# Packed attention and a routed feed-forward: contiguous probabilities, v in three transfers, another order in the first batch

## The chip, the core and the metric

One core of a Trainium2 chip. The metric is device time in microseconds (us). The engines are PE (TensorE; PEld is its weight load), DVE (VectorE), ACT (ScalarE), POOL (GpSimd) and SP (SyncE, which only issues transfers here). Before the change the median of three runs is 465.64 us (465.35 to 465.92).

## The reference

Eight batches, eight heads, 576 positions of 64 elements, 32 packing queries `p` per head:

```python
def sm_attn(qq, kk, vv):
    s = scale * np.matmul(qq, kk.transpose(0, 1, 3, 2))
    a = softmax(s)
    return np.matmul(a, vv)
p_packed = sm_attn(p, k, v)              # 32 rows a head
out = sm_attn(q, p_packed, p_packed)     # 576 rows a head
x = out, heads joined: (4608, 512)
expert = argmax(normalized x @ normalized emb.T / tau)
y = gate * (relu(x @ w1[expert]) @ w2[expert])   # experts 512 -> 1024 -> 512
```

## The kernel before, in words

A batch is worked in two groups of four heads, g = 0 and 1. Its steps are: scores of the 32 packing queries against all keys (keys are turned in 32x32 blocks by DVE in `flip`, L268), their maximum (`key_max`, L326), exponential (`key_exp`, L330) and sum; the probabilities `p1` (128 rows of 4 heads x 32 queries, 576 columns) are transposed by PE in six pieces of 96 columns (`p1_turn`, L347), copied to SBUF (`p1_evac`) and multiplied with `v` (`pack_values`, L364). So in each piece the 96 keys on the partitions of `p1T` must be those on the partitions of the `v` tile. `flip` leaves column 32c + i for key 18i + c. `key_exp` then writes each column to the place of its key's number, a step of 18 elements apart, `p1_turn` takes every sixth column, and `load_v` (L189) puts the keys 6i to 6i + 5 on partition i, in one transfer of 96 partitions.

The packed rows give a second attention over all 576 queries (`att2`, L550): scores, a softmax in two halves of 288 columns (unpack, maximum, subtraction, exponential, sum, division, transpose, and a split of the result into a high and a low part), then routing (`route`, L661), counting (`counts`, L711) and gates (`gates`, L725). The expert of a batch is guessed (`guess`, L524) to load its weights early. The feed-forward (`ffn`, L822) takes w1 through the packed rows (G), then hidden matmuls (L868) in two halves of 8, whose results ACT and DVE take out of PSUM (L872, L873), 8 small steps for the last 64 rows (L895), and 4 x 8 steps of output matmuls (L913).

Engines execute their own queues in program order, and the program's order is written out: the feed-forward of batch b is a generator with a step per matmul group, and steps of batch b + 1's attention are put between (loop at L1295). Batch 0 has no feed-forward to hide behind. `begin` (L995) does its start: loads, scores, packing, the guess and the query scores of batch 0, then, step by step, batch 1's key scores and batch 0's packed rows and logits. `PLAN` (L1238) says which steps follow each step of batch 0's feed-forward: `q` is a step of `begin`, `s` of batch 0's softmax (its order is ORDS, L1230), `a` of batch 1's attention (`att_main`, L974, which takes `att1` with `pack_slowly`, L473), `G` and `w` split a piece of G and w2 into high and low parts, `r` is a step of batch 0's routing and counting, `g` of its gates. Entry 0 runs ahead of the feed-forward; entry n + 1 follows its step n: steps 0 to 11 are the first half of hidden with both parts of G (L836, L848), 12 to 19 the second half, 20 to 27 the small steps, 28 to 59 the output matmuls.

Transfers are issued by SP in program order (`nc.sync`), a few at the start by ACT, one by POOL, and weights of later batches by POOL. PSUM has three banks `pf` (`bank`, hidden, outputs), two double banks `pt` (`turn_bank`: scores, transposes, routing) and one `pu`. Batch 1's scores are made from POOL-scaled `wy` (L1034).

## Time and profile before

| | |
|---|---|
| median of three runs | 465.64 us |
| the profiled execution | 465.4 us, of which 463.8 are the span shown |
| PE busy | 439.3 us (95%) |
| DVE, ACT, POOL busy | 301.5, 211.9, 143.1 us |
| mean granted clock of PE | 0.984 |

The span is the time from the first to the last instruction. A busy PE is one with a matmul in flight, not one at its peak. The granted clock is a share of full speed: 1.00 is 2.4 GHz, and the lower level is 1.2 GHz. In a row of the timeline the brackets hold the idle time of the engine before the row and what ended it. A name like L334 is a line of the kernel, `pt<-ident,p` says what is written from what; names with q (SPq, ACTq) are an engine's queue when it issues a transfer.

### The profile page before, as it was taken

The page shows a single profiled execution, that of the slowest core. Times are in us where ns is not written, and L with a number is a line of the kernel's source. Part 1 is how long each engine was busy: PE and PEld are TensorE (multiplying, and loading weights), DVE is VectorE, ACT ScalarE, POOL GpSimd, SP SyncE. Part 2 cuts the span into 40 slices and gives each one's busy share as a digit, 9 for nine tenths or more (in the row PEclk, how much of TensorE's full clock was granted, in tenths as well). Part 3 has the DMA queues.
Part 4 walks back from the last instruction along what each step waited for, and adds up shares of the span by engine and source line. Part 5 has one row for each costly group of instructions (what it writes and reads, how often), then busy time and mean ns, then how long its engine had stood idle before and what let it go on. Part 6 is the DMA issues. An engine that isn't in the chain of part 4 may idle for free.

```text
span 463.8 us, 10721 instructions
## 1 busy us (share of the span) xinstructions
PE 439.3 (95%) x3926; PEld 345.2 (74%) x3927; DVE 301.5 (65%) x924; ACT 211.9 (46%) x478; POOL 143.1 (31%) x182
## 2 busy tenths in 40 slices
PE   6878979999999999999999999999999999999993
PEld 5544947768788796878788786878788796879783
DVE  4366858646895589846895589936895678735500
ACT  1447651366325651376325652276324662465210
POOL 1433663041521336040531326040531327023200
PEclk9899988999999999999999999999999999999998
DMA  7659768566597575876597656876587523710022
GB/s 205 217 197 290 207 178 290 183 168 181 152 365 204 153 216 194 295 191 176 153 342 228 175 164 200 299 209 173 158 320 213 168 69 108 291 47 23 14 47 50
DMA packets 39243, 87.11 MB, mean 188 GB/s; under 512 B 11144, under 2 KB 18568, under 8 KB 39184
## 3 DMA queue, kind: packets, MB, share of 16 engines
q1 hardware_dynamic: 30752, 56.85, 43.8%
q0 software_dynamic: 7872, 29.36, 17.2%
q8 instruction: 33, 0.54, 0.5%
q10 hardware_dynamic: 560, 0.15, 0.2%
q14 instruction: 26, 0.21, 0.1%
HBM read 76.89 MB, written 9.44 MB: 186 GB/s over the span
## 4 chain that ended last, share of the span: by engine, by line
PE 83%; ACT 6%; DVE 6%; issue 2%; POOL 1%; POOLq 0%; ACTq 0%; DVEq 0%
PE pf L913 37%; PE pf L868 18%; PE pf L895 7%; PE pt L672 7%; ACT p L334 4%; PE pt L251 3%; PE pt L801 3%; PE pt L367 2%; PE pt L350 2%; DVE mx L328 1%; ACT hT L872 1%; DVE hT L873 1%; PE pt L229 1%; PE pt L1082 0%; DVE at L609 0%
## 5 line engine op out<-in xcount | busy, mean ns | idle before, releaser
L913 PE MATMUL pf<-w2s,hT 128*128 128x512 f32 (+1 forms) x792 | 190.0, 391 | 0.9 <-ACT o L1207 0.9
L913 PEld LDWEIGHTS pf<-w2s,hT 128*128 128x128 f32 x792 | 142.9, 189 | 40.1 <-issue 9.5
L777 POOL TENSOR_TENSOR w2s<-w2r,w2s 128x512 fp32r<-128x512 f32 x64 | 82.2, 1288 | 239.6 <-ACT w2s L776 214.4
L868 PE MATMUL pf<-AT,G 128*128 128x288 f32 x720 | 106.4, 299 | 0.8
L868 PEld LDWEIGHTS pf<-AT,G 128*128 128x128 f32 x720 | 97.6, 188 | 7.5 <-issue 2.8
L873 DVE SCALAR_TENSOR_TENSOR hT<-pf,hT 128x224 fp32r<-128x224 f32 (+1 forms) x128 | 52.6, 415 | 38.7 <-ACT hT L872 38.6
L872 ACT ACTIVATE hT<-pf 128x224 fp32r<-128x224 f32 (+1 forms) x128 | 47.6, 384 | 46.9 <-PE pf L868 46.1
L272 DVE STREAM_TRANSPOSE kt<-nat 128x576 f32<-128x576 f32 x56 | 40.6, 752 | 1.4 <-DMA nat<-in_k 1.4
L688 ACT ACTIVATE at<-pt 128x512 f32<-128x512 f32 (+1 forms) x40 | 23.9, 598 | 36.2 <-DVE lg L681 35.5
L776 ACT CAST w2s<-w2r 128x512 fp32r<-128x512 f32 x64 | 39.2, 615 | 2.3 <-issue 1.2
L1207 ACT ACTIVATE o<-pf,gate 128x512 f32<-128x512 f32 (+1 forms) x41 | 26.0, 635 | 28.4 <-PE pf L913 17.5
L672 PEld LDWEIGHTS pt<-ppx,AT 128*128 128x128 f32 (+1 forms) x240 | 33.1, 177 | 5.6 <-issue 1.5
L672 PE MATMUL pt<-ppx,AT 128*128 128x264 f32 (+1 forms) x240 | 36.3, 287 | 0.0
L895 PE MATMUL pf<-w2r,h 128*64 128x256 f32 x256 | 35.0, 395 | 0.0
L815 DVE TENSOR_TENSOR G<-pt,G 128x512 fp32r<-128x512 f32 x28 | 18.8, 690 | 17.3 <-ACT G L814 17.3
L681 DVE TENSOR_REDUCE lg<-pt 128x8 f32<-128x16 f32 (+1 forms) x40 | 6.7, 167 | 35.4 <-PE pt L672 35.4
L588 ACT ACTIVATE st<-st 128x576 f32<-128x576 f32 (+1 forms) x17 | 11.2, 660 | 33.8 <-DVE st L585 33.1
L334 ACT ACTIVATE p<-pt,mx 128x576 f32<-128x576 f32 x16 | 21.4, 1337 | 9.6 <-DVE mx L328 9.6
L895 PEld LDWEIGHTS pf<-w2r,h 128*64 128x64 f32 x256 | 15.7, 137 | 9.6 <-issue 4.1
L766 POOL DMA_DIRECT2D w2r<-in_moe_w x28 | 19.8, 716 | 0.0
L615 ACT CAST AT<-at 128x576 fp32r<-128x576 f32 x16 | 10.8, 674 | 19.2 <-DVE at L609 19.2
L814 ACT CAST G<-pt 128x512 fp32r<-128x512 f32 x28 | 15.9, 589 | 7.3 <-DVE G L815 4.5
(184 smaller groups left out, 460.8 us busy)
## 6 DMA issues: line engine op xcount, KB each, us to landing
nat<-in_q SPq DMA_DIRECT2D x112, 140.0 KB, 3.1
w1t<-in_moe_w POOLq DMA_DIRECT2D x14, 1024.0 KB, 7.0
w2r<-in_moe_w POOLq DMA_DIRECT2D x28, 512.0 KB, 9.8
nat<-in_k SPq DMA_DIRECT2D x96, 140.0 KB, 3.1
vn<-in_v SPq DMA_DIRECT2D x16, 576.0 KB, 6.0
out<-o SPq DMA_DIRECT2D x124, 64.0 KB, 2.7
nat<-in_k SPq DMA_DIRECT2D x4, 576.0 KB, 7.3
w1t<-in_moe_w SPq DMA_DIRECT2D x4, 512.0 KB, 5.4
```

Source lines behind the costliest of these rows:

```text
L272: nc.vector.transpose(kt.rearrange("p (c i) -> p c i", i=32), t)
L334: nc.scalar.activation(x.p1[g].rearrange(order, f=2, i=32), s1_view(x, g).rearrange("p f (c i) -> p f c i", i=32), AF.Exp, bias=x.mx[g], a ...
L672: nc.tensor.matmul(pt[:r, 512 * g : 512 * g + XW], AT[:, a, g, c * P : c * P + r], x.ppx[:, m, g], start=(i == 0), stop=(i == 2),)
L688: nc.scalar.activation(scr[:r, :, : HB * D], ptv[:r, :, 0 : HB * D], AF.Square, accum_out=ss[:r, c : c + 1])
L776: nc.scalar.copy(t[:, 0], raw)
L777: nc.gpsimd.tensor_tensor(out=t[:, 1], in0=raw, in1=t[:, 0].bitcast(F32), op=ALU.subtract)
L868: nc.tensor.matmul(pf[:, :HS], w, r, start=(n == 0), stop=(n == len(ops) - 1))
L872: nc.scalar.activation(hT[:, 0, f, cs], pf[:, :n], AF.Relu)
L873: nc.vector.scalar_tensor_tensor(out=hT[:, 1, f, cs], in0=pf[:, :n], scalar=0.0, in1=hT[:, 0, f, cs].bitcast(F32), op0=ALU.max, op1=ALU.su ...
L895: nc.tensor.matmul(pf[64 * hf : 64 * hf + 64, :256], h4[:, f], x.w2r[f // 2][:, f % 2, hf * 256 : hf * 256 + 256], start=(f == 0), stop=(f ...
L913: nc.tensor.matmul(pf[:, :w], hT[:, a, f, c * P : (c + 1) * P], x.w2s[f][:, m, at : at + w], start=(f == 0 and i == 0), stop=(f == NF - 1 ...
L1207: nc.scalar.activation(o[:, :w], pf[:, :w], AF.Copy, scale=x.gate[:, c : c + 1])
```

## The change

`load_v` puts keys 18i + 6a to 18i + 6a + 5 on partition 32a + i, for a = 0, 2, 1 in three transfers of 32 partitions; in the first batch the one with a = 2 goes by ACT. For keys `flip` writes its 18 blocks in another order, so that each stretch of 96 columns belongs to one piece; `key_exp` writes straight, and `p1_turn` reads 96 neighbouring columns. In `begin` the small loads, the query transposes and batch 1's `wy` stand elsewhere, query transposes are copied in other pieces, and batch 1's keys are turned in the blocks' new order. PLAN is another from its third entry on.

```diff
--- before.py
+++ after.py
@@ -186,12 +186,14 @@
         return t
 
 
-    def load_v(b, g):
+    def load_v(b, g, odd=nc.sync):
         t = sb.tile([P, KC * HB * D], F32, name="vn", tag="vn", bufs=2)
         t = t.rearrange("p (h w) -> p h w", h=HB)
-        nc.sync.dma_start(
-            t[:KR], v[b, g * HB : (g + 1) * HB].rearrange("h (i c) d -> i h (c d)", c=KC)
-        )
+        s = v[b, g * HB : (g + 1) * HB].rearrange("h (i c) d -> i h (c d)", c=NCB)
+        for a in (0, 2, 1):
+            (odd if a == 2 else nc.sync).dma_start(
+                t[32 * a : 32 * a + 32], s[:, :, a * KC * D : (a + 1) * KC * D]
+            )
         return t.rearrange("p h (c d) -> p h c d", c=KC)
 
     def load_p(b):
@@ -265,11 +267,18 @@
         nc.scalar.copy(dst[0], src)
         eng.tensor_tensor(out=dst[1], in0=src, in1=dst[0].bitcast(F32), op=ALU.subtract)
 
-    def flip(t, e=0):
+    def flip(t, key, e=0):
 
         kt = sb.tile([P, S], F32, name="kt", tag="kq", bufs=8)
         t = t.rearrange("p (c e d) -> p c e d", e=2, d=32)[:, :, e]
-        nc.vector.transpose(kt.rearrange("p (c i) -> p c i", i=32), t)
+        if key:
+
+            nc.vector.transpose(
+                kt.rearrange("p (n a i) -> p a n i", n=KC, i=32),
+                t.rearrange("p (a n) d -> p a n d", n=KC),
+            )
+        else:
+            nc.vector.transpose(kt.rearrange("p (c i) -> p c i", i=32), t)
         return kt
 
     def packers(x, pn):
@@ -286,7 +295,7 @@
         packers(x, pn)
         yield
         for r in range(NPR):
-            x.kT[r] = flip(nat(r))
+            x.kT[r] = flip(nat(r), True)
             yield
 
 
@@ -330,11 +339,9 @@
     def key_exp(x, g):
         x.p1[g] = sb.tile([P, S], F32, name="p1", tag="p1", bufs=2)
         x.sums[g] = sm.tile([P, 1], F32, name="sums", tag="sums")
-        order = "p (i c f) -> p f c i" if x.halves else "p (i f c) -> p f c i"
         nc.scalar.activation(
-            x.p1[g].rearrange(order, f=2, i=32),
-            s1_view(x, g).rearrange("p f (c i) -> p f c i", i=32),
-            AF.Exp, bias=x.mx[g], accum_out=x.sums[g],
+            x.p1[g].rearrange("p (f s) -> p f s", f=2), s1_view(x, g), AF.Exp, bias=x.mx[g],
+            accum_out=x.sums[g],
         )
 
     def key_sum(x, g):
@@ -347,7 +354,7 @@
     def p1_turn(x, g, pt, pl=None):
         for c in range(KC):
             to = pl[:KR, (c - 4) * P : (c - 3) * P] if pl and c >= 4 else pt[:KR, c * P : (c + 1) * P]
-            nc.tensor.transpose(to, x.p1[g][:, c::KC], ident)
+            nc.tensor.transpose(to, x.p1[g][:, c * KR : (c + 1) * KR], ident)
 
     def p1_evac(x, g, pt, w=512, spare=None, pl=None):
 
@@ -367,7 +374,7 @@
                 nc.tensor.matmul(
                     pt[32 * at : 32 * at + 32, 0:D],
                     x.p1T[g][:KR, c, 32 * at : 32 * at + 32],
-                    vt[:KR, head(g, at), c, :],
+                    vt[:KR, head(g, at), c % 3 * 2 + c // 3 if x.halves else c, :],
                     start=(c == 0),
                     stop=(c == KC - 1),
                     tile_position=(0, 32 * at),
@@ -428,7 +435,7 @@
 
         def queries():
             for r in range(NPR):
-                x.qT[r] = flip(nat(NPR + r))
+                x.qT[r] = flip(nat(NPR + r), False)
                 yield
 
         def pack():
@@ -1001,13 +1008,13 @@
         pn = sm.tile([P, NG, D], F32, name="pn4", tag="pn4", bufs=1)
         nc.scalar.dma_start(pn, p[0].rearrange("(g h) j d -> (h j) g d", g=NG))
         next(emb_gen)
+        kn = [load_whole(k[0], g) for g in range(NG)]
+        vn = [load_v(0, g, nc.scalar) for g in range(NG)]
+        nc.scalar.dma_start(itau, tau.broadcast_to([P, 1]))
+        qn = [load_whole(q[0], g) for g in range(NG)]
         ny = sm.tile([P, NG, D], F32, name="pn", tag="pn")
-        nc.scalar.dma_start(ny, p[1].rearrange("(g h) j d -> (h j) g d", g=NG))
-        kn = [load_whole(k[0], g) for g in range(NG)]
-        vn = [load_v(0, g) for g in range(NG)]
-        qn = [load_whole(q[0], g) for g in range(NG)]
+        nc.sync.dma_start(ny, p[1].rearrange("(g h) j d -> (h j) g d", g=NG))
         kn1 = [load_whole(k[1], g) for g in range(NG)]
-        nc.gpsimd.dma_start(itau, tau.broadcast_to([P, 1]))
 
         def bank():
             return ps.tile([P, 512], F32, name="pf", tag="pf")
@@ -1031,25 +1038,15 @@
         nc.vector.transpose(
             pw[:, 1].rearrange("p g e j -> p (g e j)"), pw[:, 0].rearrange("p g e j -> p (g e j)")
         )
-        wy = sb.tile([P, 2, NG, 2 * D], F32, name="wy", tag="w2s", bufs=NF)
-        nc.gpsimd.tensor_scalar(
-            out=wy[:, 0].rearrange("p g (t d) -> p g t d", t=2),
-            in0=ny.unsqueeze(2).broadcast_to([P, NG, 2, D]),
-            scalar1=SCALE, scalar2=None, op0=ALU.mult,
-        )
         for g in range(NG):
             x.s1[g] = turn_bank()
             for e in range(2):
-                kt = flip(kn[g], e)
+                kt = flip(kn[g], True, e)
                 for hf in range(2):
                     quarters(x.s1[g], pw[:, 1, g, e], kt, lambda c: head(g, c), hf, hf, e)
             if g == 0:
                 for _ in range(3):
                     next(emb_gen)
-                pu = bank()
-                for h in range(NG):
-                    nc.tensor.transpose(pu[:, h * P : (h + 1) * P], wy[:, 0, h], ident)
-                nc.scalar.copy(wy[:, 1].rearrange("p g d -> p (g d)"), pu[:, : NG * P])
         key_max(x, 0)
         key_exp(x, 0)
         key_max(x, 1)
@@ -1077,23 +1074,19 @@
         qT, kT = turned[:, 0], turned[:, 1]
         x.Tw = sb.tile([P, NG * P], F32, name="tw", tag="w2s", bufs=NF)
 
-        def turn(nat, pt, at, n):
-            for i in range(at, at + n):
+        def turn(nat, pt, blocks):
+            for at, i in enumerate(blocks):
                 nc.tensor.transpose(
-                    pt[:, (i - at) * P : (i - at + 1) * P], nat[:, i * P : (i + 1) * P], ident
+                    pt[:, at * P : (at + 1) * P], nat[:, i * P : (i + 1) * P], ident
                 )
 
         def both_rows(g):
             nc.scalar.mul(rows2[:, g], po[g][:, :D].unsqueeze(1).broadcast_to([P, 2, D]), x.rinv[g])
 
         both_rows(0)
-        qa = turn_bank()
-        turn(qn[0], qa, 0, 2)
         po.append(bank())
         pack_values(x, 1, vn[1], po[1])
         pair_rows(x, 1, po[1])
-        turn(qn[0], qa[:, 2 * P :], 2, 6)
-        nc.scalar.copy(qT[:, 0, :1024], qa)
         drain(emb_gen)
         pt = pc.tile([P, 512], F32, name="pu", tag="pu")
         for g in range(NG):
@@ -1101,23 +1094,11 @@
                 pt[:, 2 * g : 2 * g + 2], x.pp2[g].rearrange("p s d -> p (s d)"), pairs,
                 start=True, stop=True,
             )
-        qb = turn_bank()
-        turn(qn[1], qb, 0, 4)
         total = sm.tile([P, NPR], F32, name="total", tag="total", bufs=1)
         nc.vector.tensor_scalar_mul(total, pt[:, :NPR], itau)
         both_rows(1)
         g_guess = guess(x, 0, mybir.EngineType.SP, total)
         next(g_guess)
-        turn(qn[1], qb[:, 4 * P :], 4, 4)
-        pu = bank()
-        for g in range(NG):
-            turn(qn[g], pu[:, g * P :], 8, 1)
-        nc.vector.tensor_copy(qT[:, 1, :512], qb[:, :512])
-        drain(g_guess)
-        load_w1(x, x.e, 2)
-        nc.scalar.copy(qT[:, 1, 512:1024], qb[:, 512:])
-        nc.scalar.copy(qT[:, :, 1024:], pu[:, : NG * P].rearrange("p (g s) -> p g s", g=NG))
-
         pu = bank()
         for g in range(NG):
             nc.tensor.transpose(
@@ -1131,6 +1112,17 @@
                 op=ALU.mult,
             )
         nc.scalar.copy(x.Tw, pu[:, : NG * P])
+        drain(g_guess)
+        load_w1(x, x.e, 2)
+        pu = bank()
+        for g in range(NG):
+            turn(qn[g], pu[:, g * P :], (8,))
+        nc.scalar.copy(qT[:, :, 1024:], pu[:, : NG * P].rearrange("p (g s) -> p g s", g=NG))
+        for g in range(NG):
+            for n, copy in enumerate((nc.scalar.copy, nc.vector.tensor_copy)):
+                pu = bank()
+                turn(qn[g], pu, range(4 * n, 4 * n + 4))
+                copy(qT[:, g, 512 * n : 512 * n + 512], pu)
 
         def parity_scores(to, w, t, g, at):
 
@@ -1156,15 +1148,25 @@
         load_w2(x, x.e)
         prefetch(order[1, NPR] + 3)
         yield
+        wy = sb.tile([P, 2, NG, 2 * D], F32, name="wy", tag="w2s", bufs=NF)
+        nc.gpsimd.tensor_scalar(
+            out=wy[:, 0].rearrange("p g (t d) -> p g t d", t=2),
+            in0=ny.unsqueeze(2).broadcast_to([P, NG, 2, D]),
+            scalar1=SCALE, scalar2=None, op0=ALU.mult,
+        )
         pu = bank()
         for g in range(NG):
-            turn(kn1[g], pu[:, g * P :], 8, 1)
+            nc.tensor.transpose(pu[:, g * P : (g + 1) * P], wy[:, 0, g], ident)
+        nc.scalar.copy(wy[:, 1].rearrange("p g d -> p (g d)"), pu[:, : NG * P])
+        pu = bank()
+        for g in range(NG):
+            turn(kn1[g], pu[:, g * P :], (8,))
         nc.scalar.copy(kT[:, :, 1024:], pu[:, : NG * P].rearrange("p (g s) -> p g s", g=NG))
         for n in range(2 * NG):
             if n >= NG:
                 yield
             pu = bank()
-            turn(kn1[n // 2], pu, n % 2 * 4, 4)
+            turn(kn1[n // 2], pu, [m % 3 * 3 + m // 3 for m in range(n % 2 * 4, n % 2 * 4 + 4)])
             nc.scalar.copy(kT[:, n // 2, n % 2 * 512 : n % 2 * 512 + 512], pu)
         yield
         y.halves = True
@@ -1236,13 +1238,13 @@
 
 
     PLAN = (
-        "qsssqsssssssqsqssqsssqs", "s", "as", "aq", "s", "aq", "sa", "sq", "sG", "sG",
-        "qa", "qa", "a", "aGGs", "as", "as", "aw", "aw", "aw", "a",
-        "wr", "ra", "ra", "rw", "rwg", "raw", "rwa", "ra", "arg", "ar",
-        "gaa", "agaaaag", "", "ragraaararga", "a", "gar", "gr", "", "rggr", "r",
-        "ra", "", "r", "gag", "gaga", "gagrar", "grara", "ag", "a", "grrgrar",
-        "rrraggg", "", "g", "rr", "ggaaagr", "ra", "aaga", "g", "r", "rg",
-        "arr",
+        "qsssqsssssssqsqssqsssqs", "s", "s", "G", "s", "G", "s", "s", "s", "sG",
+        "G", "", "aq", "a", "aq", "as", "aq", "aws", "aqs", "awq",
+        "aw", "awr", "awr", "ar", "awr", "awr", "aw", "ar", "g", "gr",
+        "gr", "gr", "ga", "ga", "gra", "gr", "gra", "ra", "a", "a",
+        "a", "a", "a", "a", "ga", "a", "a", "aa", "a", "a",
+        "aa", "a", "aa", "a", "aa", "aa", "aa", "aa", "aa", "aa",
+        "aa",
     )
     DBL = 8
     LAG = 2
```

## Rows read from the trace of the kernel before

**Rows 1.** The page, part 1: busy us, share of the span, instructions.
```profile
PE 439.3 (95%) x3926; PEld 345.2 (74%) x3927; DVE 301.5 (65%) x924; ACT 211.9 (46%) x478; POOL 143.1 (31%) x182
```
**Rows 2.** Stages: length, busy us (instructions) by engine, granted clock, DMA share, GB/s.
```profile
8.70:16.20 7.50, 4.26 (x36) 1.70 (x36) 2.08 (x4) 1.62 (x3) 3.69 (x16) 0.77 1.07 308
16.20:26.30 10.10, 7.16 (x148) 5.84 (x148) 5.10 (x19) 4.79 (x10) 2.81 (x3) 1.00 0.23 91
...
31.60:47.90 16.30, 13.85 (x100) 8.06 (x82) 10.94 (x24) 10.31 (x24) 6.04 (x7) 1.00 1.06 291
47.90:56.30 8.40, 8.40 (x150) 8.14 (x148) 6.79 (x24) 6.19 (x16) 5.80 (x5) 1.00 0.77 206
...
71.40:101.90 30.50, 29.64 (x165) 22.84 (x159) 20.72 (x57) 12.89 (x27) 7.89 (x11) 0.96 0.73 236
...
154.50:207.00 52.50, 52.03 (x478) 41.47 (x477) 38.28 (x111) 25.22 (x58) 16.28 (x20) 1.00 0.71 215
...
64.80:71.40 6.60, 3.80 (x47) 1.30 (x45) 4.14 (x18) 1.19 (x3) 4.79 (x7) 0.66 0.45 128
```
**Rows 3.** Timeline of PE, 155.5 to 175: start, us, operation, count, idle before.
```profile
156.64 4.59 PE L868 MATMUL pf<-AT,G 128*128 128x288 f32 x30
161.07 0.82 PE L350 MATMUL pt<-ident,p 128*96 128x128 f32 x6
162.22 0.91 PE L350 MATMUL pt<-ident,p 128*96 128x128 f32 x6 [0.33 <-ACT p L334]
162.88 5.29 PE L868 MATMUL pf<-AT,G 128*128 128x288 f32 x36
```
**Rows 4.** Waits of PE from 100 us on: total us, times, longest.
```profile
PE pt L350 <- ACT p L334: 2.0, 6, 0.3
```
**Rows 5.** Groups of ACT by shape: count, busy us, mean ns, idle before.
```profile
L334 ACT ACTIVATE p<-pt,mx 128x576 f32<-128x576 f32 x16 | 21.4, 1337 | 9.6 <-DVE mx L328 9.6
...
L588 ACT ACTIVATE st<-st 128x576 f32<-128x576 f32 x15 | 10.3, 686 | 33.8 <-DVE st L585 33.1 <-POOL st L585 0.7
```
**Rows 6.** Groups of PE's weight loads by shape, same columns.
```profile
L350 PEld LDWEIGHTS pt<-ident,p 128*96 128x96 f32 x94 | 11.5, 180 | 5.6 <-ACT p L334 4.8 <-issue 0.7
...
L396 PEld LDWEIGHTS pu<-ident,pp 128*128 128x128 f32 x14 | 1.9, 138 | 0.4
```
**Rows 7.** Groups of DVE by shape, same columns.
```profile
L272 DVE STREAM_TRANSPOSE kt<-nat 128x576 f32<-128x576 f32 x56 | 40.6, 752 | 1.4 <-DMA nat<-in_k 1.4
```
**Rows 8.** DMA issues, first 60 us: count, KB, median us to landing.
```profile
vn<-in_v SPq DMA_DIRECT2D x4, 576.0 KB, 10.8
```
**Rows 9.** Timeline of all engines, start of the kernel to the first hidden matmul.
```profile
6.56 2.14 PE L229 MATMUL pt<-kt,pw 32*32 32x288 f32 x32 [0.15 <-DVE kt L272]
...
11.02 0.87 POOL L1035 TENSOR_SCALAR wy<-pn 128x256 f32<-128x256 f32 x1 [8.43 <-DMA pn<-in_p]
...
12.31 3.81 PE L229 MATMUL pt<-kt,pw 32*32 32x288 f32 x32
...
26.27 1.21 PE L1141 MATMUL pt<-spare,tw 64*32 64x288 f32 x32 [1.51 <-ACT tw L1133]
26.39 2.14 SPq L758 DMA_DIRECT2D w1t<-in_moe_w  x4
...
29.28 0.46 ACT L588 ACTIVATE st<-st 128x288 f32<-128x288 f32 x1
...
33.42 1.24 PE L868 MATMUL pf<-at,g 128*128 128x288 f32 x4 [0.68 <-ACT g L848]
```
**Rows 10.** Waits of PE from 30 to 100 us.
```profile
PE pu L714 <- DVE m L420: 2.5, 1, 2.5
...
PE pf L913 <- ACT o L1207: 0.9, 1, 0.9
```
**Rows 11.** Timeline of DVE, 71 to 86: softmax of batch 1, first and last.
```profile
71.53 0.85 DVE L574 STREAM_TRANSPOSE st<-pt 128x288 f32<-128x288 f32 x2 [1.40 <-PE pt L251]
...
84.41 0.74 DVE L620 TENSOR_TENSOR AT<-at,AT 128x576 fp32r<-128x576 f32 x1
```

## Prediction, made before the changed kernel was run

> **What bounds the kernel now.** I read the busy shares first, then stages of the span, then PE's waits, then the timeline. PE is busy 95% of the span [rows 1], and PE's busy time alone does not say what an edit is worth, so the span is cut into stages [rows 2]. From 154.5 to 207.0 us, one batch, PE is busy 52.03 of 52.50 us at full clock: the other engines matter there only where they hold PE up, 0.47 us a batch. The first 102 us are different. From 8.70 to 16.20 PE is busy 4.26 of 7.50 us and the granted clock is 0.77; from 31.60 to 47.90 it has 2.45 us of plain idle time, with DVE at 10.94 and ACT at 10.31 us; from 64.80 to 71.40 it is idle 2.80 us and its clock is 0.66, which lasts into the next stage (0.96 over 30.5 us). So an edit pays either in the first batch's stages, or through the small hold-up in each later batch.
>
> The hold-up of later batches is seen on PE's timeline [rows 3]. Thirty matmuls of L868 start at 156.64 and the next stretch of L868 at 162.88, with twelve transposes of L350 between: 6.24 us. In the next stretch 36 matmuls take 5.29, 0.14 each, and a transpose follows another at (0.91 - 0.27)/5 = 0.13, so the same work would need about 30 x 0.14 + 12 x 0.11 to 0.13 = 5.5 to 5.8. What is lost is 0.5 to 0.75 us, of which 0.33 is a wait on the exponential of L334, the only wait for another engine that the waits of PE after 100 us name (2.0 us, 6 times) [rows 4].
>
> **The change part by part.**
>
> **Exponential (key_exp).** It has its output rows made contiguous; its input was already read in stretches of 288. It takes 1337 ns now, where the other exponential of the same 128x576, written without gaps, takes 686 [rows 5]. I take 0.65 us less, by that row; the bounds are 0 (if the writes were not the cause) and 0.75. A batch has two, each ahead of ReLUs on ACT that free PE's banks. The wait of 0.33 goes, and part of the bank waits in front of it: 0.33 to 0.75 a batch, I take 0.55. Batches 2 to 7 make 6 x 0.55 = 3.3 us. ACT's next late result would be the ReLU of L872, which then runs 0.65 us earlier.
>
> **Probability transposes.** Their weights were read with a step of six elements and become contiguous; the load takes 180 ns against 138 for a contiguous 128x128 [rows 6]. But the transposes follow each other at 0.11 to 0.13 us in either case, so I count nothing; bounds 0 and 12 x 0.04 = 0.5 us a batch.
> The Trainium skill (Advanced Engine Details and Errata, SBUF Cachelines) says that accesses which leave a 16-byte line each time pay a penalty. By it the 42 ns of each load would be saved, some 3 us over six batches; the pitch of the rows speaks against it.
>
> **Key flips.** 32x32 blocks are written at another place each, 28 flips in the main loop. The duration is 752 ns [rows 7]; bounds are no change and, if placement of blocks cost what the step cost the exponential, twice that. A block still writes 32 neighbours, as the contiguous case does: nothing.
>
> **v in three transfers.** Twelve transfers for every four of before, so about 0.4 us more of SP's issue each; 2 x 2 more a batch, 1.6 us on a queue that mostly waits for stores. PE waits for three landings in place of one. v lands 10.8 us after issue at the start [rows 8], is then needed at 14 us and later: I take nothing, bounds 0 and 1 us once. In the first batch one of three goes by ACT's queue, ahead of the activation of the embeddings, which has slack.
> At the start that piece, 2 x 192 KB, 0.39 MB, is in flight with the second half of the keys; at the 308 GB/s of 8.70 to 16.20 [rows 2] that is 1.3 us, so the keys come 0 to 1.3 us later; I take 0.5. The Trainium skill (DMA: Bandwidth & Descriptors, Issuing engines are not separate DMA queues) says that such transfers share one set of engines, so a second queue saves issue time alone: by it the delay is the full 1.3 us, and the sum would be 0.8 us worse.
>
> **Start.** Today POOL's scaling for batch 1 (L1035) waits for a small load until 11.02, PE waits for it, and the second group's 32 score matmuls then run from 12.31 in 3.81 us where the first took 2.14 [rows 9]. The scaling moves behind the first batch's query scores, so the second group ends at about 11.8 and not 16.1: 4.3 us. The exponential's 0.65 comes on top. The sixteen query transposes in front of the guess go behind it, 16 x 0.11 = 1.8 us at most. The weights' load, issued at 26.39, I expect at 19.7; the query scores, at 26.27, at 20.6, since the eighteen transposes and their five copies now stand directly ahead of them (2.4 us as I count it, ACT and DVE side by side). Then a new wait: the moved scaling stands on POOL behind the first half's subtraction, about 2 us after the scores, and PE's transposes of it, its copy and the copies of batch 1's keys stand on ACT ahead of the first softmax exponential. That one starts 3.0 us after the scores today (29.28) and I expect 5.5: 2.5 us given back. The first hidden matmul, at 33.42 today, comes at 30.4: **3.0 us**, bounds 1 and 5.5 (scaling fully hidden).
>
> **First batch, first half of hidden (31.6 to 47.9).** Batch 1's steps leave it: two maxima and small work, 2.9 us of DVE; two exponentials and copies, about 5.8 of ACT. What is left on DVE in order (two copies of G, eight hT, the second half's softmax, one split) comes to 9.2 us, and with the wait for POOL's subtraction at its head I get 12.2 us for the stage of 16.3. Twelve transposes and the logits, 2.2 us of PE's work, only move: **2.0 us**, bounds 0 and 3.
>
> **Second half of hidden.** Batch 1's steps come in here. Today ACT is busy 6.19 of 8.40 us [rows 2]; with two shorter exponentials, two copies of p1T and two splits of w2, it gets 9.3 against PE's 8.9: **1.0 us lost**, bounds 0 and 2.
>
> **Routing and after.** PE waits 2.5 us at L714 [rows 10], behind a copy of batch 1's logits; with batch 1's logits moved to later, and PE given two steps of L913 ahead of the counting, DVE's chain lies beside PE's work. Idle time 2.8 and the clock (3.80 us at 0.66, 30.5 at 0.96, so about 1.3 and 1.2) make 5.3; I take **4.6 us**, bounds 2 and 5.3. The gates are finished some three steps ahead of the first store, and the wait of 0.9 at L913 [rows 10] goes: **0.9 us**.
>
> **End of the first batch.** DVE's softmax of batch 1 takes from 71.53 to 85.15, 13.6 us [rows 11], with the keys' flips, 4 x 0.75 and the packers, 3.5 us, behind it. The new plan has about 19 steps of L913 between query scores and the first route matmul, at 0.72 us each 13.8 us. So DVE's softmax just fits, and the second routing matmuls wait for their banks behind the flips: 1.5 us, and 0.5 where G of batch 1 is ready late: **2.0 us lost**, bounds 0 and 5. Loads of batch 1's weights come later, but have over 15 us.
>
> **Sum.** 3.3 + 3.0 + 2.0 - 1.0 + 4.6 + 0.9 - 2.0 = 10.8 us. The profiled execution took 465.4 (span 463.8 and 1.6 around it), so 454.6; the median of the runs is 0.24 above it, so 454.9, said as 455.0.
>
> **The rivals.**
> - **The first batch gives nothing beyond its start.** Batch 1's chain, moved by ten steps, ends behind PE's work at the route, and eats what routing and gates gave. For it: 13.8 us of cover against 13.6 and more of DVE. Against it: DVE has pauses while ACT computes exponentials. Then 3.0 + 3.3 remain: 459.1. Chance 0.2.
> - **More than forecast.** POOL's scaling costs nothing, DVE fits: 2.5 + 2.0 + 1.0 more, 449.4. Chance 0.12.
> - **The exponential does not get faster,** so that the change doesn't do there what it says (its cost was the reading of two banks): 3.3 and some 0.7 of the start are gone: 459. Chance 0.05.
> - **Slower: the low clock.** The new start leaves PE with short bursts between 12 and 28 us, without the query transposes that fill it now. Today 8.70 to 16.20 was granted 0.77 after PE had next to nothing to do between 8.70 and 12.31, and the score matmuls took 1.78 times as long [rows 9]. PE has about 10 us of work on the chain from there to the first hidden matmul and 7 to 9 in the stage behind it; at the lower level of 1.2 GHz, by 0.78 us for each, that costs up to 8 and, half hidden, 4. With 12 lost against 10.8 the time is 466.8. It decides once the low clock covers nearly all of 10 to 40 us. Against it: 16.20 to 26.30, as loosely filled (7.16 of 10.10 us), had full clock [rows 2]. Chance 0.08.
> - Key flips at twice the time would add 3 us of DVE a batch to 38.28 of 52.50 [rows 2], which PE needs only partly: 462 to 468, chance 0.03.
>
> **How the numbers follow.** The forecast has 0.52. Its own bounds run from 449 to 460. The range takes in the first rival and the second nearly whole: 449.0 to 461.5, leaving out the slow cases and a little of the fast. About 0.2% is what a measurement of this kernel can tell from no change; faster 0.89 (the first four cases), slower 0.09 (the low clock and a third of the flips' case), same 0.02 (the rest of that case).
>
> **What would show it.** Right: L334 near 0.69 us; a batch's period near 52.0 and no wait at L350; the second group's scores done by 12 us; first w1 issue near 20; first hidden matmul near 30; ffn of batch 1 (hidden) starting near 95 where it starts at 101.9. Wrong: L334 unchanged, a low clock between 10 and 40 us, waits of PE for DVE at the routing of batch 1.

## The result, and the profile after

The changed kernel took 460.14 us as the median of four runs (458.36 to 460.86), the kernel before 465.72; the ratio is 0.9875, 95% interval 0.9847 to 0.9904. It is faster by 5.6 us, where 10.7 were forecast: inside the range, and half of what the sum promised. A second measurement (run after2 below) gave 0.985 [0.982, 0.988].

The profiled execution took 458.36 us, its span is 456.8, 7.0 shorter than before; it was the fastest of the four, and the one with the highest granted clock (0.988, the others 0.980 and 0.981). In the changed file most lines stand some seven further down: the exponential L334 is L342, the transposes L350 are L357, the hidden matmuls L868 are L875, the outputs L913 are L920, the key scores L251 are L253.

**Later batches.** First the groups by shape, of ACT, PE's weight loads and DVE (the columns of [rows 5]):
```profile
L342 ACT ACTIVATE p<-pt,mx 128x576 f32<-128x576 f32 x16 | 11.8, 741 | 7.3 <-DVE mx L337 7.3
...
L357 PEld LDWEIGHTS pt<-ident,p 128*96 128x96 f32 x94 | 10.4, 126 | 1.7 <-ACT p L342 1.1 <-POOL rq_t L109 0.6
...
L281 DVE STREAM_TRANSPOSE kt<-nat 128x576 f32<-128x576 f32 x28 | 21.3, 764 | 0.0
L276 DVE STREAM_TRANSPOSE kt<-nat 128x576 f32<-128x576 f32 x28 | 19.1, 736 | 0.0
```
The exponential fell from 1337 to 741 ns, the weight load from 180 to 126, and the key flips (L276), whose blocks now go elsewhere, cost no more than the query flips, which stayed. The timeline of PE, where [rows 3] answers:
```profile
154.39 4.21 PE L875 MATMUL pf<-AT,G 128*128 128x288 f32 x30
158.44 1.47 PE L357 MATMUL pt<-ident,p 128*96 128x128 f32 x12
159.67 5.29 PE L875 MATMUL pf<-AT,G 128*128 128x288 f32 x36
```
The stretch of 6.24 us is 5.28 now, and the wait inside it is gone. A whole batch, in the view of stages, is 51.60 where it was 52.50 [rows 2]:
```profile
152.30:203.90 51.60, 51.55 (x478) 41.44 (x478) 38.27 (x111) 24.48 (x59) 16.32 (x20) 1.00 0.73 219
```

**First batch.** Its stages, in the columns of [rows 2]:
```profile
28.40:41.70 13.30, 11.09 (x78) 6.59 (x58) 10.28 (x21) 7.34 (x15) 5.65 (x5) 1.00 1.03 271
41.70:52.50 10.80, 10.38 (x167) 9.53 (x165) 7.04 (x25) 8.82 (x26) 5.81 (x7) 1.00 0.45 132
52.50:61.60 9.10, 9.10 (x71) 5.75 (x64) 6.25 (x15) 5.68 (x16) 7.43 (x8) 1.00 0.23 67
61.60:93.60 32.00, 31.21 (x208) 23.04 (x207) 23.14 (x74) 11.99 (x27) 11.24 (x16) 1.00 0.88 272
93.60:101.20 7.60, 3.89 (x44) 1.72 (x42) 3.12 (x6) 2.45 (x5) 0.35 (x1) 0.79 0.63 173
101.20:111.20 10.00, 10.00 (x68) 9.99 (x66) 5.00 (x13) 5.04 (x14) 0.00 (x0) 0.82 0.37 107
```
The routing stage has full clock and hardly an idle PE. The loss sits in the last two rows: PE is busy only 3.89 of 7.60 us in the first, and the granted clock is 0.79 there and 0.82 in the next. All engines there, by the timeline:
```profile
91.95 6.19 SPq L1215 DMA_DIRECT2D out<-o  x9
...
93.64 0.95 PE L875 MATMUL pf<-AT,G 128*128 128x288 f32 x6
...
95.71 0.69 ACT L1209 ACTIVATE o<-pf,gate 128x512 f32<-128x512 f32 x1 [1.73 <-DMA out<-o]
96.30 0.58 ACT L821 CAST G<-pt 128x512 fp32r<-128x512 f32 x1
96.91 0.69 DVE L822 TENSOR_TENSOR G<-pt,G 128x512 fp32r<-128x512 f32 x1 [2.79 <-ACT G L821]
97.63 0.59 ACT L821 CAST G<-pt 128x512 fp32r<-128x512 f32 x1 [0.76 <-DVE G L822]
98.11 0.42 ACT L879 ACTIVATE hT<-pf 128x288 fp32r<-128x288 f32 x1
...
98.86 0.18 DVE L726 TENSOR_REDUCE cnt<-pu 1x8 f32<-1x40 f32 x1
...
99.08 2.15 PE L253 MATMUL pt<-kt,pw 64*32 64x288 f32 x24 [3.71 <-DVE cnt L726]
...
101.16 5.86 PE L875 MATMUL pf<-AT,G 128*128 128x288 f32 x30
```
Read it upwards from the last row but one. PE waits 3.71 us for the counts of L726, a small reduction that DVE could have done at 94.8. It stands on DVE's queue behind two subtractions for G (L822), these wait for ACT's copies (L821), and ACT had been waiting 1.73 us for an output buffer: there are two, and a store had not left yet. Why not, SP's own queue tells:
```profile
83.65 5.42 SPq L178 DMA_DIRECT2D nat<-in_q  x12
89.18 1.32 SPq L194 DMA_DIRECT2D vn<-in_v  x3
90.59 7.55 SPq L1215 DMA_DIRECT2D out<-o  x12
```
Fifteen loads for a later batch stand ahead of the stores. An output that ACT had copied at 83.09 left from 90.59 on, and its buffer was the one ACT wanted at 94. In the kernel before the same kind of loads stands ahead of the stores too:
```profile
87.49 5.47 SPq L178 DMA_DIRECT2D nat<-in_q  x12
...
93.53 12.86 SPq L1213 DMA_DIRECT2D out<-o  x16
```
But no output copy of ACT waited more than 0.24 us there: the outputs came later against the queue (the third copy at 95.70, here at 83.09).

**The balance of the 7.0 us.** The hidden matmuls of batch 1 start 8.3 us earlier (93.64 against 101.93). The stretch of 30 hidden matmuls shown above, in the second batch after, is only 2.25 earlier (154.39 against 156.64): 6.0 were given back between. That is a net figure, since a batch's gain by the shorter exponential, some 0.95, lies in this stretch too, so 7.0 were lost in it: 3.7 by the wait above; 2.6 by the lower clock (the 24 score matmuls took 2.15 us, 1.17 at full clock in the run drain below, and the thirty hidden matmuls behind them 5.86, where the thirty shown above took 4.21); 0.7 is not traced further. The batches behind it, five of the six that gain, then add 4.75.

### The profile page after: what moved, and what is told of

It is laid out like the page before. It is cut to its first block, busy times and chain, and to the rows that moved or that the text cites. A ratio compares the mean times of both kernels' runs of the same rounds, so it can differ in the third digit from the quotient of the medians.

```text
span 456.8 us, 10781 instructions
## 1 busy us (share of the span) xinstructions
PE 434.9 (95%) x3926; PEld 345.6 (76%) x3927; DVE 302.9 (66%) x925; ACT 204.9 (45%) x478; POOL 142.6 (31%) x181
## 4 chain that ended last, share of the span: by engine, by line
PE 84%; DVE 6%; ACT 4%; DMA 2%; issue 1%; POOL 1%; SPq 0%; ACTq 0%; DVEq 0%; POOLq 0%
PE pf L920 36%; PE pf L875 22%; PE pf L902 6%; PE pt L679 6%; PE pt L253 3%; PE pt L808 2%; PE pt L374 2%; PE pt L357 2%; DMA pn<-in_p 1%; DMA out<-o 1%; DVE kt L276 1%; ACT p L342 1%; DVE hT L880 0%; DVE at L616 0%; PE pt L231 0%
## 5 line engine op out<-in xcount | busy, mean ns | idle before, releaser
L920 PE MATMUL pf<-w2s,hT 128*128 128x512 f32 (+1 forms) x792 | 189.2, 390 | 0.0
L920 PEld LDWEIGHTS pf<-w2s,hT 128*128 128x128 f32 x792 | 142.0, 188 | 38.3 <-issue 9.4
L875 PE MATMUL pf<-AT,G 128*128 128x288 f32 x720 | 106.9, 302 | 0.7 <-DVE h L885 0.4
L875 PEld LDWEIGHTS pf<-AT,G 128*128 128x128 f32 x720 | 99.2, 191 | 6.7 <-issue 3.2
L879 ACT ACTIVATE hT<-pf 128x224 fp32r<-128x224 f32 (+1 forms) x128 | 48.6, 385 | 49.5 <-PE pf L875 48.1
L822 DVE TENSOR_TENSOR G<-pt,G 128x512 fp32r<-128x512 f32 x28 | 18.9, 690 | 17.9 <-ACT G L821 17.9
L595 ACT ACTIVATE st<-st 128x576 f32<-128x576 f32 (+1 forms) x17 | 11.2, 660 | 31.1 <-DVE st L592 30.4
L281 DVE STREAM_TRANSPOSE kt<-nat 128x576 f32<-128x576 f32 x28 | 21.3, 764 | 0.0
L746 ACT ACTIVATE lg<-lg 128x40 f32<-128x40 f32 x8 | 1.9, 237 | 39.6 <-DVE lg L742 39.6
L821 ACT CAST G<-pt 128x512 fp32r<-128x512 f32 x28 | 15.9, 588 | 7.4 <-DVE G L822 4.8
```

What stands on the lines that cost most here:

```text
L281: nc.vector.transpose(kt.rearrange("p (c i) -> p c i", i=32), t)
L875: nc.tensor.matmul(pf[:, :HS], w, r, start=(n == 0), stop=(n == len(ops) - 1))
L879: nc.scalar.activation(hT[:, 0, f, cs], pf[:, :n], AF.Relu)
L920: nc.tensor.matmul(pf[:, :w], hT[:, a, f, c * P : (c + 1) * P], x.w2s[f][:, m, at : at + w], start=(f == 0 and i == 0), stop=(f == NF - 1 ...
```

## The experiments

The line numbers in these rows are those of each kernel's own file, and ratios are against the kernel before on the same chip.

**1 and 2. The layout alone, the order alone.** layout is the kernel before with the contiguous exponential, key flips by the new index and v in three pieces on SP; order_only is the change without these.
```diff
-            x.p1[g].rearrange(order, f=2, i=32),
-            s1_view(x, g).rearrange("p f (c i) -> p f c i", i=32),
-            AF.Exp, bias=x.mx[g], accum_out=x.sums[g],
+            x.p1[g].rearrange("p (f s) -> p f s", f=2), s1_view(x, g), AF.Exp, bias=x.mx[g],
+            accum_out=x.sums[g],
...
```


> The kernel before with the contiguous probability rows, the new flips and v in three transfers (all by SP), and nothing else. Theory: the exponential alone makes each later batch shorter, 51.6 us a batch where before has 52.5, and the start by about 0.7 us; so 5.4 to 6.5 us less than before, 459.2 to 460.3. Rival: three transfers for one of v delay what stands behind them on SP, and eat part of it: a period over 52.0 and a time of 462 or more.

> The changed kernel with the old probability layout, the old flips and v in one transfer: only the start and the plan are new. Theory: period 52.5 as before; the first batch reaches the first hidden matmul of batch 1 some 6 to 7 us earlier than before (before 101.9), and gives most of it back in the wait behind the output stores and the low clock after it: 463.5 to 466. Rival: the three transfers of v in front of the stores on SP make that wait, so with one transfer it is gone or under 1.5 us, and the time is 461 or less.

Measured: layout 457.57 us, ratio 0.983 [0.979, 0.987], below the range expected of it: its start came 1.8 to 2.5 us earlier and not 0.7, and the rest of the first batch gained 2 us too (66.5 and 66.7 from its first hidden matmul to batch 1's in two profiles, 68.5 before); order_only 465.59, 0.999 [0.997, 1.002], as expected. The measured gain is the layout's. Not that the order did nothing on its way: in order_only batch 1's hidden matmuls start at 94.11, 7.8 us early, and then PE stands still and the clock falls (timeline of PE, then the stage from 90 to 110 us):
```profile
100.01 1.67 PE L251 MATMUL pt<-kt,pw 64*32 64x288 f32 x20 [4.17 <-DVE cnt L719]
```
```profile
90.00:110.00 20.00, 15.52 (x134) 11.14 (x133) 8.71 (x21) 10.12 (x22) 2.59 (x2) 0.83 0.58 153
```
v is loaded in one piece there, so the pieces did not make the stall.

**3. G's copies ahead of the last stores (drain).** The changed kernel, with two lines at the end of the first batch:
```diff
+        if late:
+            drain(after.w1g)
         for t in last:
             store(*t)
```


> The changed kernel, but at the end of the first batch's feed-forward the copies of batch 1's G are put ahead of the last two output stores on ACT and DVE. Theory: the stall of PE at batch 2's key scores (3.7 us) comes from ACT, which waits 1.7 us for an output buffer with two of G's copies behind it; it falls under 1 us, the clock stays up behind it, and the time falls by 4 to 6.5 us to 453.6 to 456. Rival: G is late because batch 1's steps end late in the plan; then the wait stays over 2.5 us and the time within 1 us of the changed kernel's 460.1.

Measured: 455.13, 0.977 [0.973, 0.981]. PE's timeline and the same stage:
```profile
97.99 1.17 PE L253 MATMUL pt<-kt,pw 64*32 64x288 f32 x24 [0.83 <-DVE cnt L726]
```
```profile
90.00:110.00 20.00, 19.12 (x201) 15.36 (x204) 12.94 (x36) 13.18 (x34) 4.70 (x4) 1.00 0.70 188
```
The wait is 0.83 and the clock full. From the start of batch 1's hidden matmuls to the next hidden stretch, after the key scores, it is 3.67 us (95.42 to 99.09) where the changed kernel needs 7.52. As the theory had it: the order of ACT's queue, with the buffer wait at its head, was the stall.

**4. The exponential with gaps again (strided_exp).** All else as in the change; its transposes read contiguous rows, so the probabilities meet rows of v that are not theirs. That leaves the same work.


> The changed kernel with the exponential writing its columns 18 apart again, while the transposes of the probabilities read neighbouring columns; the probabilities then meet rows of v that aren't theirs. Theory: the exponential's duration makes the gain of a later batch: L342 back at 1.34 us, period 52.4 to 52.6, time 465 to 467. Rival: the transposes' weight loads (180 ns to 138) carry a good part: period under 52.2 although the exponential is slow, time under 464.

Measured: 464.58, 0.996 [0.994, 0.999]. ACT's and the weight loads' groups, and a batch:
```profile
L343 ACT ACTIVATE p<-pt,mx 128x576 f32<-128x576 f32 x16 | 21.4, 1338 | 8.4 <-DVE mx L337 8.4
...
L359 PEld LDWEIGHTS pt<-ident,p 128*96 128x96 f32 x94 | 10.2, 126 | 5.5 <-ACT p L343 4.4 <-POOL ery L117 1.1
```
```profile
162.60:215.10 52.50, 52.04 (x478) 41.44 (x478) 38.29 (x112) 25.25 (x57) 16.35 (x19) 1.00 0.73 220
```
The weight load is short (126) and the batch is 52.50 again, as in the kernel before; the time is a little under the theory's 465 to 467. So the 0.90 us a batch come with the exponential. The stretch of thirty hidden matmuls and twelve transposes that took 6.24 us before and 5.28 in the change takes 6.18 here (156.18 to 162.36, by PE's timeline), so the 54 ns of each load bring at most 0.06 us of it while the exponential is slow. The opposite pair, a short exponential with the long load, was not run.

**5 and 6. Start and plan apart.** old_plan is the change with the kernel before's PLAN; layout_newplan is layout with the new PLAN and the old start. The exchange, as old_plan has it:
```diff
-        "qsssqsssssssqsqssqsssqs", "s", "s", "G", "s", "G", "s", "s", "s", "sG",
+        "qsssqsssssssqsqssqsssqs", "s", "as", "aq", "s", "aq", "sa", "sq", "sG", "sG",
...
```


> The changed kernel (new start, new layout) with PLAN of before. Theory: the plan's tail is what loses, the start gains: no PE wait over 1 us at batch 2's key scores, first hidden matmul near 30.2, and 455.5 to 457.5, at or a little under the layout alone (457.6). Rival: the new start gains nothing that the old plan can use: 457.5 to 459.

> The kernel before with the new layout and the new PLAN, but with the old start. Theory: the stall of 3.7 us and the low clock after it belong to the plan, so it comes here too, with the start of the layout alone (first hidden matmul 30.9): 460 to 462, about 3 us more than the layout alone. Rival: the stall needs the new start; then 455 to 457.

Measured: old_plan 456.99 (455.74 to 460.04), 0.978 [0.973, 0.984], in the theory's range, though its first hidden matmul came at 33.63 and not near 30.2; layout_newplan 459.21, 0.983 [0.978, 0.989], under its range, with the stall that its theory named. The intervals overlap; the traces part them. From the first hidden matmul to batch 1's, the old plan needs 66.5 and 66.7 us (the two profiles of layout), 67.0 in early_oldplan below, and 68.7 in old_plan, whose profiled execution, the slowest of its four, was granted 0.71 and 0.95 from 20 to 40 us. The new one needs 63.4 in each of after, after2, drain, early_wy and layout_newplan: the plan does gain some 3.2. From there to the next hidden stretch the old plan needs 2.2, the new one 7.5 (after), 7.1 (after2) and 6.9 (layout_newplan, with the buffer wait and 3.66 on the counts). The lower clock behind it belongs to the account: from the first hidden matmul to the thirty hidden matmuls of batch 2, layout needs 120.3 and 120.4 us, and after 124.2, after2 123.3, layout_newplan 123.1. So this plan as it stands loses 2.7 to 3.9 us against the old one, and with drain's two lines (118.7) it gains 1.7.

**7. Batch 1's scaling sooner (early_wy).** drain, with POOL's scaling (wy) and its transposes put ahead of the query transposes; both are taken out further down.
```diff
...
+        nc.gpsimd.tensor_scalar(
+            out=wy[:, 0].rearrange("p g (t d) -> p g t d", t=2),
+            in0=ny.unsqueeze(2).broadcast_to([P, NG, 2, D]),
+            scalar1=SCALE, scalar2=None, op0=ALU.mult,
+        )
         drain(g_guess)
         load_w1(x, x.e, 2)
+        pu = bank()
+        for g in range(NG):
+            nc.tensor.transpose(pu[:, g * P : (g + 1) * P], wy[:, 0, g], ident)
...
```


> The kernel with G's copies ahead of the stores, and batch 1's scaled p made on POOL and turned on PE ahead of the query transposes, not behind the query scores. Theory: PE's wait of 1.9 us for POOL at L1159 goes and the first softmax exponential comes some 2 us earlier; first hidden matmul near 28.2 where the clock is full (30.2 with the step behind the scores); 452.5 to 454, about 2 us under the kernel with the copies ahead (455.1). Rival: the small load of p is late or ACT's extra copy delays the query scores as much: within 0.6 us of 455.1.

Measured: 452.42, 0.970 [0.965, 0.975], the fastest of all. The wait for POOL is 0.4 instead of 1.9, the first hidden matmul at 27.68:
```profile
17.71 0.44 PE L1127 MATMUL pf<-ident,wy 128*128 128x128 f32 x2 [0.41 <-POOL wy L1118]
...
27.68 4.15 PE L875 MATMUL pf<-at,g 128*128 128x288 f32 x16 [0.68 <-ACT g L855]
```
That is 2.5 and 1.3 us earlier than in the change's two profiles (after and after2), which also had full clock from 12 to 28 us. Against drain (455.13) the time fell by 2.7, but part of this may be the clock: over their spans drain's runs were granted 0.987 to 0.995, these 0.990 to 0.997, and the two were measured on different chips.

**8. The first batch's stores by POOL's queue (pool_stores).**
```diff
-                    nc.sync.dma_start(
+                    nc.gpsimd.dma_start(
```


> The changed kernel with batch 0's output stores issued by POOL and not by SP. Theory: ACT's wait of 1.7 us for an output buffer comes from SP, which issues twelve loads of q and three of v ahead of the store that frees it; by POOL the store goes at once, the stall of PE falls under 1.5 us and the time to 454 to 456.5. Rival: the wait is the store's own time to land; then the stall stays over 2.5 us and the time at 459 or more.

Measured: 458.59, 0.983 [0.978, 0.988]; neither of the two expectations came true. PE's waits, and two output copies of ACT:
```profile
PE pt L253 <- DVE cnt L726: 1.9, 1, 1.9
PE pt L679 <- ACT at L695: 1.8, 1, 1.8
```
```profile
87.74 0.69 ACT L1209 ACTIVATE o<-pf,gate 128x512 f32<-128x512 f32 x1 [3.33 <-DMA out<-o]
...
95.84 1.27 ACT L1209 ACTIVATE o<-pf,gate 128x512 f32<-128x512 f32 x2
```
With SP's loads out of the way the two last copies wait for nothing, and PE's wait on the counts falls from 3.7 to 1.9 (G's copies still stand behind them). But POOL's queue holds stores too, between 76 and 88 us, while its own issue waits for w1t, w2r and ACT: the buffer wait comes earlier and longer, 3.33, and PE pays 1.8 at the routing for it. The stores were moved from one full queue to another.

**9 and 10. The change and the layout, side by side.**


> The changed kernel, unaltered, on the same chip as the layout alone, because the two have so far been compared only through the kernel before. If the new order is worth nothing on top of the layout: ratio 0.982 to 0.990, and equal to layout2 within 0.003. If the new order costs time: over layout2 by 0.004 or more (0.0043 by the first measurements). If it gains: under it by 0.004 or more. Its trace should repeat the stall of 3.7 us on the counts and the output buffer's 1.7.

> The layout alone, again, beside the full change. By the first measurement 0.983; equal to the full change within 0.003 if the order is worth nothing, below it by 0.004 or more if the order costs.

Measured: after2 459.04, 0.985 [0.982, 0.988]; layout2 456.47, 0.979 [0.975, 0.983]. By the medians the order costs 2.6 us on top of the layout. The two profiled executions (456.22 and 456.24) don't show it: there after2, with full clock from 12 to 20 us where layout2 was granted 0.79, has its first hidden matmul 2.7 ahead (29.00 against 31.67), and the plan gives that back. The stall is there again, 3.96 us.

**11. early_wy with the old plan (early_oldplan).**


> The best kernel so far (drain of G ahead of the stores, scaling for batch 1 early) with the old plan of steps for the first batch. If the new plan is worth its promised time once its stall is removed (first half of hidden, routing, gates: 2.0 - 1.0 + 4.6 + 0.9, less what batch 1 waits at the end), this is slower than that kernel's 0.970 by 2 us or more: 0.975 to 0.982. If the plan is worth nothing even then, 0.967 to 0.972.

Measured: 455.23, 0.976 [0.973, 0.979]: slower by 2.8, though on another chip and with intervals that touch. By the stages of 5 and 6 the plan's share is 2.1 (67.0 and 2.2 against 63.4 and 3.7); this run's profiled start was granted 0.82 and 0.75 from 12 to 28 us and early_wy's 1.00, so the rest may be that. The new plan is worth its place once its stall is out.

**12. early_wy with q ahead of v on SP's queue (early_q).** In the change, SP issues q's loads at 8.33 us, not at 3.08, because the four pieces of v hold the queue 4.01 us and q's loads then wait about 2.5 more, by SP's waits for a landing of v; PE then waited 1.37 at the query transposes. That wait is in the profiles of after and drain (1.15), not in those of after2 and early_wy, though q left as late there.
```diff
-        vn = [load_v(0, g, nc.scalar) for g in range(NG)]
         nc.scalar.dma_start(itau, tau.broadcast_to([P, 1]))
         qn = [load_whole(q[0], g) for g in range(NG)]
+        vn = [load_v(0, g, nc.scalar) for g in range(NG)]
```


> The best kernel so far with the four loads of q issued on the queue of SP ahead of the pieces of v. If the wait of PE for q at the query transposes (1.4 us in the changed kernel) is on the path to the first hidden matmul, that matmul comes 0.5 to 1.5 us sooner than 27.7 and the ratio is 0.966 to 0.969; if the scaling and the softmax set the path, or v's later landing takes its place, first hidden stays within 0.5 us and the ratio at 0.970.

Measured: 456.35, 0.979 [0.976, 0.982], so 3.9 us slower than early_wy; both expectations missed. v now lands late, and the clock is low (PE's timeline, then two stages, the clock third from the end):
```profile
15.44 1.47 PE L374 MATMUL pf<-vn,p1T 96*32 96x64 f32 x48 [2.00 <-DMA vn<-in_v]
17.62 1.51 PE L374 MATMUL pf<-vn,p1T 96*32 96x64 f32 x48 [0.71 <-DMA vn<-in_v]
...
33.61 4.15 PE L875 MATMUL pf<-at,g 128*128 128x288 f32 x16 [0.68 <-ACT g L855]
```
```profile
12.00:20.00 8.00, 4.71 (x108) 4.09 (x109) 2.51 (x11) 1.79 (x6) 2.19 (x2) 0.72 0.97 247
20.00:28.00 8.00, 7.36 (x69) 5.98 (x70) 3.44 (x11) 2.42 (x6) 1.44 (x2) 0.64 0.49 168
```
The first hidden matmul is 5.9 us later than in early_wy: 2.7 are the two waits for v, the rest the lower clock. Whether the waits brought the clock down isn't shown: drain was granted 0.85 and 0.72 in these two stretches without them. Of the two loads, v is the one that the first 20 us must have early.

## Why the prediction was right or wrong

**Right in sign and in the main mechanism, and near in size partly by luck.** In the profiled execution the parts come to 3.2 (start) + 0.6 (hidden) + 4.5 (routing and gates) - 7.0 (end) + 5.7 (six later batches at 0.95) = 7.0 us. The later batches gave 2.4 more than their term, and that covered over a third of what the end lost beyond its term. The median gained 1.4 less than this execution, whose start had full clock.

The exponential was faster by its contiguous writes: 0.60 us of the 0.65 taken from the row of L588. The Trainium skill (Advanced Engine Details and Errata, SBUF Cachelines) says that accesses which leave a 16-byte line each time pay a penalty; the trace agrees for ACT's writes (1337 to 741 ns) and for the weight load (180 to 126). That the shorter load would shorten a batch was refused on the pitch of the transposes, and strided_exp bears that out. Key flips at no cost: right, 736 ns. The delay of the keys by v's piece on ACT's queue, 0.5 us, was not seen, and so not the 1.3 of its upper bound either: their second half is flipped at 7.94, before at 8.73. The Trainium skill (DMA: Bandwidth & Descriptors, Issuing engines are not separate DMA queues) says that transfers share one set of engines whoever issues them; no run here isolates that, because q's loads left 5.2 us later than before.

**Start: 3.0 forecast, 3.2 measured** in the profiled execution (first hidden matmul 30.21, forecast 30.4), the second group's scores done at 10.9 and w1 issued at 18.10. The wait for POOL's scaling came as the new wait that was named (1.9). Not foreseen was that SP's queue is held by v's pieces, which delayed q. But layout alone, with the old start, has its first hidden matmul at 30.94 and 31.67, 1.8 to 2.5 us ahead of before, where the step had put 0.65 for the exponential. In part that is the clock: the second group's score matmuls, 3.81 us before, took 2.14 and 3.12 there. So the new order's moves were worth the rest, 0.7 (after against the earlier of the two) to 2.7 us (after2 against the later), and that where the clock was full.

**Both halves of hidden: 1.0 net forecast, 0.6 measured** (24.70 to 24.10 us). The first half gave 3.0, the second lost 2.4, above its bound of 2: PE itself has 10.38 us of work there, since the twelve transposes and the logits taken out of the first half land in it.

**Routing and gates: 5.5 forecast.** From the end of both halves of hidden (56.30 before, 52.50 now) to batch 1's hidden matmuls it was 45.63 and is 41.14: 4.5 less, where 4.0 stood, with the 1.5 for banks freed late, which the prediction counts to the end of the batch, taken off. The wait of 2.5 is 0.38, the gates' wait gone, the clock full.

**The step that failed: the end of the first batch.** It said 2.0 lost, bounds 0 and 5, by DVE's softmax and flips. Lost were 7.0 behind the start of batch 1's hidden matmuls alone (6.0 net of a batch's gain), where only the 0.5 for a late G stood behind that point; this is above the bound for the whole step, and DVE was not late by its own work: it waited for ACT, ACT for an output buffer, the buffer for SP's queue. The step priced G late at 0.5 and never asked when the stores, on a queue full of loads, give their buffers back once the outputs come earlier. drain shows it by taking ACT's part away: with its two lines the stretch is 5.5 shorter (55.26 from the start of batch 1's hidden matmuls to batch 2's thirty, in the change 60.75), so the end loses 1.5, inside what the step had priced. pool_stores, by taking SP's part, moved the wait.

**Later batches: mis-sized.** 0.55 a batch was taken, 0.90 to 0.96 measured: 4.75 us for five batches, so some 5.7 for the six for which 3.3 stood. The upper bound of 0.75 was too low because it took 5.5 us for the work without any hold-up: thirty matmuls at 4.2 and twelve transposes at 1.3. With the exponential early they take 4.05 and 1.23, 5.28 together.

**The rivals.** The first came out nearest in time (459.1), not in its mechanism: routing and gates kept what they gave, and what ate it was the wait behind the stores. The low clock of the start, held for a slower case, is real but did not make the kernel slower. In the profiles of kernels with the new start the stretch from 12 to 28 us has full clock in some and not in others: drain was granted 0.85 and 0.72, and its first hidden matmul came at 32.03, 1.8 later than in the change. The changed kernel's timed runs had 0.980 to 0.992 over their spans, the slowest times at the low end. Where in an unprofiled run the clock was lost stays open, and with it how much of the 2.6 us between layout2 and after2 is the plan's stall and how much the start.

## What to carry to other kernels

When a plan brings results forward, follow their buffers back to the queue that empties them: a store behind fifteen loads on SP's queue stopped ACT, through ACT DVE, and through DVE PE. Work that the next stage needs belongs on its engine's queue ahead of work that can wait for a buffer; two lines did that here and were worth 4 to 5 us. And measure the parts of a change alone: this one's layout beat the whole of it, by 2.6 us.

## What was not expected of the hardware

One kernel's executions differ by which stretches of the first 30 us are granted the lower clock: layout's profile has 1.00 from 12 to 20 us, layout2's, the same kernel, 0.79, and the first hidden matmul came 0.73 us later. And a wait can cost more than its length: behind the stalls of 3.7 to 4.2 us in after, after2 and order_only the next 24 score and thirty hidden matmuls took 2.6, 1.6 and 1.7 us longer than at full clock, and where drain's wait is 0.83 the clock stays at 1.00.
